# Moving a router's maximum and normalisation to later steps of a two-product expert kernel, with four banks for the second product in two steps

## The chip, the cores and the metric

The kernel runs on one core of one Trainium2 chip. The metric is the device time of one execution in microseconds (us); lower is better. TensorE is called PE below, VectorE DVE, ScalarE ACT, GpSimd POOL, and SyncE, which issues the DMAs, SP.

## What is computed

Attention feeds a layer with a cosine gate, and that feeds a mixture of eight experts whose router is normalised by rows and columns eight times. The change touches the last part:

```python
def _moe2_ref(x, w_gate, w1, w2):        # x 2304x512, w_gate 512x8, w1 8x512x1024, w2 8x1024x512
    logits = x @ w_gate
    logits = logits - logits.max()
    P = np.exp(logits)
    for _ in range(8):
        P /= P.sum(1, keepdims=True) + 1e-09
        P /= P.sum(0, keepdims=True) + 1e-09
        P *= N / E
    out = np.zeros((N, D))
    for e in range(E):
        h = np.maximum(x @ w1[e], 0.0)
        out += P[:, e:e + 1] * (h @ w2[e])
```

## The kernel before

**Steps.** The experts' part is a loop over 16 half-experts `u` (4 to 19) and three blocks of 768 tokens `j`. One pass is called a step here; step 0 is the first, so `s` is 12 plus the step, and there are 48. Three steps in a row, one for each `j`, make one half-expert; steps 0 to 5 are expert 0, steps 6 to 11 expert 1. A step has four groups `k` = 0 to 3 on PE. Each group starts with the first product of this step (x times w1; `g1_mult`, L763), in which seven multiplications stand for eight (Strassen's scheme): multiplications 0 and 6 in group 0, 1 and 5 in group 1, 4 and 3 in group 2, 2 in group 3. Then come the parts of the second product (h times w2; `g2_mult`, L837) of the step before. A multiplication is 12 matmuls of 384 columns, so a step has 7 x 12 of each product, 168 in all.

**PSUM banks.** The first product uses banks 0 to 3 in two pairs, X and Y (`two_banks(x)` and `two_banks(1 - x)`), which change roles with each step: what is Y in one step is X in the next, and the next step's first matmuls overwrite it. In group 3 only X is in use. The second product has two chains. With the table `WIDE` they use banks 4, 5 and 6, 7; with `NARROW` the second chain has bank 6 alone, so that bank 7 is free, and its parts 5, 3 and 2 are cut in halves of six matmuls. Between two halves bank 6 has to be read out (`g2_add`, L857 on DVE, or L859 on ACT where a block is written for the first time).

**Order.** Each engine works through its instructions in the order in which the code is written. Beside the two products the following ran in the first steps. `x_steps` (steps 0 to 2) makes the high and low halves of the seven combinations of x on ACT and DVE (`x_low` is L670, `x_sum` L652). `split_h` makes the halves of h (ACT L741, DVE L746), `first_sums`, `second_sum` and `third_sum` are L812, L817, L821. Group 3 adds a term to X (L805), then rectifies it on ACT.

**The router.** `logits` (matmuls L923, transposes L931, sums L911) and `sinkhorn` are generators. Each call of `step_side()` runs one of them to its next `yield`. Before the change there are four calls in every group: at its start, in the middle of its first product (`between`), and after its first and second part of the second product. `sinkhorn` takes the maximum `mx` (L939), transposes it on PE into bank 7 (L943), reduces it to `top` (L945), spreads it with a matmul (L949) and takes the exponentials (L952). One of the eight normalisations is: row sums `rs` and their reciprocals (DVE L956 to L958), their use and the column sums `cs` (L960, L964), a matmul with ones (L969) that adds them over the partitions, reciprocals `rc` (L971, L972) and their use (L974). At the end `by_e` (L979) is transposed on PE (L985) and stored to DRAM (`pd`).

**The use of the router.** `pb_load` (L886) reads 768 of these factors from `pd` into one of three tiles `pb`, spread over the partitions, on SP's queue. Expert 0 is multiplied with them after its second product (`scale_first`, L892, four DVE instructions per block, in steps 5 to 7); the experts after it at the rectification on DVE (`relu_scaled`, L775), from step 6 on.

**The end.** In the last step `out_tile` (L897 transposes into bank 7, L903 copies out) runs twice after all parts of groups 0, 1 and 2.

Of the kernel before, what the change touches and what calls it, by code (L numbers as in the profile page):

```python
# [18 lines left out]
P = 128  # L19
# [5 lines left out]
U1 = 2048 // 512  # L25
U2 = E * FE // 512
NU = U1 + U2
HC = 288

HT = 384  # L30
NJ = 3
# [73 lines left out]
def tile_kernel(ctx: ExitStack, tc: tile.TileContext, qT, kT, v, pT, w_in, w_out, w_gate, w1, w2, out):  # L105
    nc = tc.nc
# [718 lines left out]
    def split_h(s, m):  # L825
        h_high(s, m)
        h_low(s, m)
# [53 lines left out]
        for r, d in outs:  # L881
            g2_add(j, r, d, banks[chain], tiles)

    def pb_load(e, j):
        row = e * NT + 2 * HT * j
        nc.sync.dma_start(out=pb[j], in_=p_flat[row:row + 2 * HT].partition_broadcast(P))  # L886

    def scale_first(j, k):
        r, d = k // 2 + 1, k % 2 + 1
        scale = pb[j][:, HT * (2 - r):HT * (3 - r)].unsqueeze(1).to_broadcast([P, 2, HT])  # L890
        block = out_block(j, r, d)
        nc.vector.tensor_tensor(out=block, in0=block, in1=scale, op=ALU.mult)  # L892

# [12 lines left out]
    def out_tile(j, i, b):  # L906
        out_turn(j, i, b)
        out_store(j, i, b)
# [7 lines left out]
    def logits():  # L916
        copies = (l_sb, raws[4][:, 0:HT])
        for c in range(2 * NJ + 1):
            if c < 2 * NJ:
                ps = bank[:, 6 + c % 2, :]  # L920
                x = acc_cols(HT * c, HT)
                for k in range(KD):
                    nc.tensor.matmul(  # L923
                        ps[32 * k:32 * k + 32, 0:HT], lhsT=wgs[:, k, :], rhs=x[:, k, :],
                        start=True, stop=True,
                    )
                nc.scalar.copy(copies[c % 2], ps[:, 0:HT])
            if c > 0:
                ps, l = bank[:, 7 - c % 2, :], copies[1 - c % 2]
                for i in range(TQ):  # L930
                    nc.tensor.transpose(ps[:, P * i:P * i + P], l[:, P * i:P * i + P], ident)  # L931
                lg_sum(lg[:, TQ * c - TQ:TQ * c, :], ps, TQ)
            yield
            if c < 2 * NJ:
                yield

    def sinkhorn():
        mx = small.tile([P, 1], F32, tag="mx", name="mx")
        nc.vector.tensor_reduce(mx, lg, axis=AX.XY, op=ALU.max)  # L939
        yield  # L940
        yield
        t_ps = bank[:, 7, :]
        nc.tensor.transpose(t_ps[0:1, 0:P], mx, ident)  # L943
        top = small.tile([1, 1], F32, tag="top", name="top")
        nc.vector.tensor_reduce(top, t_ps[0:1, 0:P], axis=AX.X, op=ALU.max, negate=True)  # L945
        yield
        yield
        b_ps = bank[:, 7, :]
        nc.tensor.matmul(b_ps[:, 0:1], lhsT=ones[0:1, :], rhs=top, start=True, stop=True)  # L949
        nmx = small.tile([P, 1], F32, tag="nmx", name="nmx")  # L950
        nc.vector.tensor_copy(nmx, b_ps[:, 0:1])
# [2 lines left out]
        for k in range(8):  # L954
            rs = small.tile([P, NT // P], F32, tag="rs", name="rs")
            nc.vector.tensor_reduce(rs, prob, axis=AX.X, op=ALU.add)  # L956
            nc.vector.tensor_scalar(rs, rs, EPS, None, ALU.add)
            nc.vector.reciprocal(rs, rs)  # L958
            yield
            nc.vector.tensor_tensor(  # L960
                out=prob, in0=prob, in1=rs.unsqueeze(2).to_broadcast([P, NT // P, E]), op=ALU.mult
            )
            cs = small.tile([P, E], F32, tag="cs", name="cs")
            nc.vector.tensor_reduce(cs, prob.rearrange("p t e -> p e t"), axis=AX.X, op=ALU.add)  # L964
            yield
            yield
            yield
            c_ps = bank[:, 7, :]
            nc.tensor.matmul(c_ps[:, 0:E], lhsT=ones, rhs=cs, start=True, stop=True)  # L969
            rc = small.tile([P, E], F32, tag="rc", name="rc")  # L970
            nc.vector.tensor_scalar(rc, c_ps[:, 0:E], EPS, None, ALU.add)  # L971
            nc.vector.reciprocal(rc, rc)  # L972
            yield
            nc.vector.scalar_tensor_tensor(  # L974
                out=prob, in0=prob, scalar=float(NT) / E,
                in1=rc.unsqueeze(1).to_broadcast([P, NT // P, E]), op0=ALU.mult, op1=ALU.mult,
            )
# [19 lines left out]
    def step_side():  # L997
        while side:
            try:
                next(side[0])  # L1000
                return
            except StopIteration:
                side.pop(0)

    with tc.manual_schedule():
# [188 lines left out]
        for u in range(U1, NU):  # L1194
            for j in range(NJ):
                s = NJ * u + j
                first_unit = u == U1
                narrow = s <= NJ * U1 + 4 or s == NJ * NU - 1
                banks = ((4, 5), (6, 6)) if narrow else ((4, 5), (6, 7))
                if pair_no and not narrow:  # L1200
                    banks = banks[::-1]
                x = counts["chunk"] % 2
                counts["chunk"] += 1
                for k in range(4):
                    def between():
                        if prev is not None and k == 1:
                            h_low(s - 1, 3)
                        if NJ * (U1 + 1) + 2 <= s < NJ * (U1 + 2) + 2:
                            scale_first(s - NJ * (U1 + 1) - 2, k)
                        step_side()  # L1210

                    step_side()
                    if prev is not None:
                        if k == 0:
                            split_h(s - 1, 5)
# [7 lines left out]
                    if k == 2:  # L1223
                        first_sums(u, j, x)
                    parts = (NARROW if narrow else WIDE)[k] if prev is not None else ()
                    if prev is None and k < 3:
                        in_g2(n1 - 3 + k)
                        in_acc(n1 - 3 + k)
                        if k == 2:
                            split_h(s, 1)  # L1230
                    for n in range(max(2, len(parts))):
                        if n < len(parts):
                            g2_part(*prev, parts[n], banks)
                            if n == 0:
                                if k == 0:
                                    split_h(s - 1, 6)
                                elif k == 1:
                                    split_h(s - 1, 7)
                                    split_h(s - 1, 2)
                                elif k == 2:  # L1240
                                    split_h(s, 1)
                        if n < 2:
                            step_side()
                            if first_unit and 2 * k + n < 7 and 7 * j + 2 * k + n + 3 < 7 * NJ + 2:
                                x_steps(7 * j + 2 * k + n + 5, [halves(t) for t in pb])
                    if s == NJ * NU - 1 and k < 3:
                        out_tile(0, 2 * k, 7)
                        out_tile(0, 2 * k + 1, 7)

                    if first_unit and j == 0:  # L1250
                        for _ in range((2, 1, 0, 0)[k]):
                            next(preps[u], None)
# [2 lines left out]
                    if u + 1 < NU:  # L1255
# [7 lines left out]
                        if j == 2 and k == 3:  # L1263
                            makes[u + 1] = t_make(u + 1)
                            next(makes[u + 1])
                    if s == NJ * (U1 + 1) + 1 and k == 3:
                        for i in range(NJ):
                            pb_load(0, i)
                    if NJ * (U1 + 1) + 2 <= s < NJ * (U1 + 2) + 2:
                        if k == 3:  # L1270
                            pb_load(1, s - NJ * (U1 + 1) - 2)
                    if u >= U1 + 3 and k == 0:
                        if j > 0 and u % 2 == 1 and (u - U1) // 2 + 1 < E:
                            pb_load((u - U1) // 2 + 1, j - 1)
# [87 lines left out]
```

## Time and profile before

| | us |
|---|---|
| median of 3 runs | 1864.05 (1863.54 to 1865.42) |
| the profiled execution, its own time | 1863.85 |
| its span | 1861.8 |
| PE busy in the span | 1817.7 |
| DVE busy | 1482.7 |
| ACT busy | 829.5 |
| POOL busy | 834.3 |

The span runs from the first to the last instruction; 2.05 us of the execution's time lie outside it. A busy share is a mean over stages, and matmuls overlap, so what counts for PE is how long a step of 168 matmuls takes.

### The profile page before, as it was taken

How to read it: one execution, taken by the hardware profiler on the slowest of the kernel's cores; microseconds unless marked ns; L12 is line 12 of the kernel's file. 1: busy time of each engine (PE TensorE's matmuls, PEld its weight loads, DVE VectorE, ACT ScalarE, POOL GpSimd, SP SyncE). 2: the span in 40 equal slices, each digit the busy share in tenths (PEclk: the TensorE clock that was granted, in tenths of full speed). 3: DMA queues.
4: the chain of work that ended last, by engine and by line, in shares of the span. 5: the costliest groups of instructions: out<-in, count | busy, mean ns of one | idle time of the engine just before them, and what ended most of it. 6: DMA issues, size and time to landing. Idle time of an engine off the chain costs nothing.

```text
span 1861.8 us, 29725 instructions
## 1 busy us (share of the span) xinstructions
PE 1817.7 (98%) x11751; PEld 1775.0 (95%) x11751; DVE 1482.7 (80%) x1614; ACT 829.5 (45%) x1247; POOL 834.3 (45%) x542
## 2 busy tenths in 40 slices
PE   6999999997999999999999999999999999999998
PEld 4799999987899999999999999999999999999998
DVE  5867777558777988888888888888888888888876
ACT  5877777655544333333333333333333333333333
POOL 3544555543344454454545454444444544545420
PEclk9999999998999999999999999999999999999999
DMA  8511111035556766766766666666767666666652
GB/s 290 182 47 46 57 47 58 9 119 175 178 189 234 239 217 218 238 199 213 236 219 209 209 227 221 218 207 220 235 211 233 228 210 218 209 228 224 210 185 104
DMA packets 220839, 345.20 MB, mean 185 GB/s; under 512 B 13836, under 2 KB 190748, under 8 KB 220700
## 3 DMA queue, kind: packets, MB, share of 16 engines
q1 hardware_dynamic: 220700, 343.29, 55.4%
q8 instruction: 94, 1.54, 0.3%
q14 instruction: 45, 0.37, 0.1%
HBM read 321.93 MB, written 21.31 MB: 184 GB/s over the span
## 4 chain that ended last, share of the span: by engine, by line
PE 92%; DVE 4%; ACT 1%; issue 1%; DMA 1%; POOL 0%; ACTq 0%; SPq 0%; DVEq 0%; POOLq 0%
PE bank L837 37%; PE bank L763 36%; PE bank L606 11%; PE bank L547 2%; PE bank L548 2%; PE bank L549 2%; DMA k<-kT 1%; PE bank L483 1%; DVE hreg L746 1%; DVE xl L670 0%; PE bank L897 0%; DVE acc L857 0%; PE bank L308 0%; DVE pb L652 0%; ACT acc L859 0%
## 5 line engine op out<-in xcount | busy, mean ns | idle before, releaser
L837 PE MATMUL bank<-hreg,thi 128*128 128x384 f32 x2016 | 516.8, 337 | 6.7 <-DVE acc L857 5.0
L763 PE MATMUL bank<-xl,xh 128*128 128x384 f32 x1344 | 453.1, 337 | 3.8 <-DVE xl L670 3.8
L763 PE MATMUL bank<-xh 128*128 128x384 f32 x1344 | 454.7, 338 | 0.0
L763 PE MATMUL bank<-xh,xl 128*128 128x384 f32 x1344 | 452.7, 337 | 0.0
L857 DVE TENSOR_TENSOR acc<-bank,acc 128x768 f32<-128x768 f32 (+1 forms) x344 | 314.6, 916 | 116.6 <-PE bank L837 113.9
L837 PEld LDWEIGHTS bank<-hreg,thi 128*128 128x128 f32 x2016 | 366.6, 188 | 8.2 <-DVE acc L857 5.9
L746 DVE TENSOR_TENSOR hreg<-raw,hreg 128x768 fp32r<-128x768 f32 x252 | 337.4, 1346 | 23.6 <-ACT hreg L741 23.6
L837 PE MATMUL bank<-hreg,tlo 128*128 128x384 f32 x1008 | 340.0, 337 | 0.0
L741 ACT CAST hreg<-raw 128x768 fp32r<-128x768 f32 x252 | 207.3, 835 | 275.7 <-DVE raw L821 129.3
L243 POOL TENSOR_TENSOR tlo<-raw,thi 128x512 fp32r<-128x512 f32 x112 | 169.1, 1515 | 262.7 <-ACT thi L242 242.5
L813 POOL TENSOR_TENSOR raw<-raw,raw 128x768 f32<-128x768 f32 x48 | 88.8, 1851 | 399.4 <-DVE raw L812 399.4
L763 PEld LDWEIGHTS bank<-xl,xh 128*128 128x128 f32 x1344 | 253.8, 189 | 5.1 <-DVE xl L670 5.1
L763 PEld LDWEIGHTS bank<-xh 128*128 128x128 f32 x1344 | 253.3, 188 | 0.6 <-issue 0.6
L763 PEld LDWEIGHTS bank<-xh,xl 128*128 128x128 f32 x1344 | 253.5, 189 | 0.0
L711 POOL TENSOR_TENSOR xl<-wraw,xh 128x512 fp32r<-128x512 f32 x112 | 189.0, 1700 | 130.2 <-ACT xh L710 130.2
L837 PEld LDWEIGHTS bank<-hreg,tlo 128*128 128x128 f32 x1008 | 189.8, 188 | 0.0
L606 PE MATMUL bank<-hreg,whi 128*128 128x288 f32 x1024 | 187.9, 295 | 0.2 <-DVE rbuf L587 0.2
L775 DVE SCALAR_TENSOR_TENSOR raw<-bank,pb 128x768 f32<-128x768 f32 x168 | 160.0, 952 | 21.0 <-PE bank L763 16.5
L837 PE MATMUL bank<-slot,thi 128*128 128x384 f32 x672 | 172.6, 338 | 0.7 <-DVE acc L857 0.7
L606 PEld LDWEIGHTS bank<-hreg,whi 128*128 128x128 f32 x1024 | 153.1, 188 | 2.0 <-DVE rbuf L587 1.1
L242 ACT CAST thi<-raw 128x512 fp32r<-128x512 f32 x112 | 68.1, 619 | 156.6 <-POOL raw L246 155.2
L563 POOL TENSOR_TENSOR hreg<-rbuf,hreg 128x576 fp32r<-128x576 f32 x64 | 91.9, 1438 | 96.3 <-ACT hreg L557 86.7
(153 smaller groups left out, 2680.5 us busy)
## 6 DMA issues: line engine op xcount, KB each, us to landing
xh<-xd SPq DMA_DIRECT2D x315, 384.0 KB, 3.4
xl<-xd SPq DMA_DIRECT2D x315, 384.0 KB, 4.1
raw<-w SPq DMA_DIRECT2D x32, 512.0 KB, 6.3
wraw<-w SPq DMA_DIRECT2D x30, 512.0 KB, 6.2
pb<-pd SPq DMA_DIRECT2D x24, 384.0 KB, 5.6
raw<-w_in SPq DMA_DIRECT2D x16, 512.0 KB, 4.4
raw<-w_out SPq DMA_DIRECT2D x16, 512.0 KB, 3.7
xd<-xh SPq DMA_DIRECT2D x21, 384.0 KB, 3.1
```

Of the source, the lines that this page charges most:

```text
L242: nc.scalar.copy(hi, src)
L243: nc.gpsimd.tensor_tensor(out=lo, in0=src, in1=hi.bitcast(F32), op=ALU.subtract)
L563: nc.gpsimd.tensor_tensor(out=lo, in0=r, in1=hi.bitcast(F32), op=ALU.subtract)
L606: nc.tensor.matmul(ps[:, di, 0:HC], lhsT=lhsT, rhs=rhs, start=(n in (0, 6)), stop=(n in (17, 23)),)
L711: nc.gpsimd.tensor_tensor(out=lo, in0=src, in1=hi.bitcast(F32), op=ALU.subtract)
L741: nc.scalar.copy(hi, step_tiles(s)[H_SRC[m]])
L746: nc.vector.tensor_tensor(out=lo, in0=step_tiles(s)[H_SRC[m]], in1=hi.bitcast(F32), op=ALU.subtract)
L763: nc.tensor.matmul(dst, lhsT=w, rhs=t[:, k, :], start=start and k == 0 and w is a and t is th, stop=k == 1 and w is bq, skip_group_check=True,
L775: nc.vector.scalar_tensor_tensor(out=out, in0=src, scalar=0.0, in1=scale, op0=ALU.max, op1=ALU.mult)
L813: nc.gpsimd.tensor_tensor(out=r21, in0=r11, in1=r21, op=ALU.subtract)
L837: nc.tensor.matmul(dst, lhsT=w, rhs=t[:, p, :], start=start and p == 0 and w is a and t is hh, stop=p == 1 and w is bq, skip_group_check=True,
L857: nc.vector.tensor_tensor(out=dst, in0=src, in1=dst, op=ALU.add)
```

## The change

1. **Fewer calls.** `step_side()` runs four times per group only in step 0 and from step 3 on (`busy`); in steps 1 and 2 it runs once, in the middle of group 3. The number of yields is changed to match: the logits take all of step 0, `mx` is reduced in group 3 of step 0, its transpose and `top` stand in group 3 of step 1, the spreading and the exponentials in group 3 of step 2. The eight normalisations have four calls each instead of five, so that they fill steps 3 and 4, one per group; `by_e` is copied, transposed and stored in group 0 of step 5. The column sums now have two calls between them and their matmul, where they had three.
2. **Banks.** The transposed and the spread maximum go to the first bank of Y (`free["bank"]`), which group 3 does not use. `NARROW` now stands for steps 3, 4, 5 and the last instead of 1 to 4 and the last.
3. **Step 0.** The last three `in_g2` (the end of the layer before) move from ahead of both side calls of a group to between them.
4. **Factors.** The loads of `pb` and the scalings move to steps 5 to 8, with one load more (7 instead of 6), and group 2 has two scalings.
5. **The end.** The two `out_tile` of a group follow one part each.

```diff
-    def scale_first(j, k):
+    def scale_first(j, k, t):
...
-            yield
-            if c < 2 * NJ:
+            for _ in range((2, 2, 2, 2, 3, 1, 0)[c]):
                 yield
...
+    free = {}
...
-        yield
-        yield
-        t_ps = bank[:, 7, :]
+        for _ in range(4):
+            yield
+        t_ps = bank[:, free["bank"], :]
...
             cs = small.tile([P, E], F32, tag="cs", name="cs")
             nc.vector.tensor_reduce(cs, prob.rearrange("p t e -> p e t"), axis=AX.X, op=ALU.add)
-            yield
             yield
             yield
             c_ps = bank[:, 7, :]
...
-                narrow = s <= NJ * U1 + 4 or s == NJ * NU - 1
+                narrow = s in (NJ * U1 + 3, NJ * U1 + 4, NJ * U1 + 5, NJ * NU - 1)
...
+                    now = s - NJ * U1
+                    busy = now == 0 or now >= NJ
...
-                        if NJ * (U1 + 1) + 2 <= s < NJ * (U1 + 2) + 2:
-                            scale_first(s - NJ * (U1 + 1) - 2, k)
+                        if 2 * NJ <= now < 3 * NJ:
+                            for n in ((0,), (1,), (2, 3), ())[k]:
+                                scale_first(now - 2 * NJ, n, pb[(2, 2, 0)[now - 2 * NJ]])
+                        if busy or k == 3:
+                            free["bank"] = 2 * (1 - x)
+                            step_side()
+
+                    if busy:
                         step_side()
...
-                    if prev is None and k < 3:
-                        in_g2(n1 - 3 + k)
-                        in_acc(n1 - 3 + k)
-                        if k == 2:
-                            split_h(s, 1)
                     for n in range(max(2, len(parts))):
+                        if n == 1 and prev is None and k < 3:
+                            in_g2(n1 - 3 + k)
+                            in_acc(n1 - 3 + k)
+                            if k == 2:
+                                split_h(s, 1)
...
                         if n < 2:
-                            step_side()
+                            if s == NJ * NU - 1 and k < 3:
+                                out_tile(0, 2 * k + n, 7)
+                            if busy:
+                                step_side()
...
-                    if s == NJ * (U1 + 1) + 1 and k == 3:
-                        for i in range(NJ):
-                            pb_load(0, i)
-                    if NJ * (U1 + 1) + 2 <= s < NJ * (U1 + 2) + 2:
-                        if k == 3:
-                            pb_load(1, s - NJ * (U1 + 1) - 2)
+                    for when, group, e, i, t in (
+                        (5, 3, 1, 0, 0), (5, 3, 0, 0, 2), (5, 3, 1, 1, 1), (6, 2, 0, 1, 2),
+                        (7, 0, 0, 2, 0), (7, 2, 1, 2, 2), (8, 2, 1, 0, 0),
+                    ):
+                        if (now, k) == (when, group):
+                            pb_load(e, i, pb[t])
```

The lines below show what stands on an engine in the built program, first before and then after the change; line numbers are those of each kernel. On DVE, at the end of step 1, from the readout of part 2 on (`acc` L857; `xl` and `pb` are the splitting of x, `rs`, `rc`, `prob`, `cs` the router's), before:

```order
L971 TENSOR_SCALAR rc<-bank 128x8
L972 RECIPROCAL rc<-rc 128x8
L670 TENSOR_TENSOR xl<-pb_3999,xh 128x2x384
L652 TENSOR_TENSOR pb_3998<-acc_1628,pb_3997 128x768
L857 TENSOR_TENSOR acc_101<-bank,acc_101 128x384
L974 SCALAR_TENSOR_TENSOR prob<-prob,rc 128x144
L956 TENSOR_REDUCE rs<-prob 128x18
L957 TENSOR_SCALAR rs<-rs 128x18
L958 RECIPROCAL rs<-rs 128x18
L805 TENSOR_TENSOR bank<-bank,base 128x2x384
L960 TENSOR_TENSOR prob<-prob,rs 128x144
L964 TENSOR_REDUCE cs<-prob 128x8
```

And after, at the same place, up to the first two instructions of step 2:

```order
L857 TENSOR_TENSOR acc_101<-bank,acc_101 128x2x384
L670 TENSOR_TENSOR xl<-pb_3999,xh 128x2x384
L652 TENSOR_TENSOR pb_3998<-acc_1628,pb_3997 128x768
L805 TENSOR_TENSOR bank<-bank,base 128x2x384
L948 TENSOR_REDUCE top<-bank 1x1
L670 TENSOR_TENSOR xl<-acc_1628,xh 128x2x384
L746 TENSOR_TENSOR slot<-raw_4411,slot 128x768
L817 TENSOR_TENSOR raw_4411<-raw_4411,raw_4408 128x768
```

The normalisation's instructions are gone from there, and the reduction to `top`, which reads the first bank of Y, stands behind L805. On SP's queue, at the end of step 5 (`xh`, `xl` are loads of x, `raw32` loads of w2, `pb` the factors), before:

```order
L682 DMA xh_73<-xd_94 128x2x384
L682 DMA xl_74<-xd_94 128x2x384
L218 DMA raw32_6026<-w2 128x2x512
L218 DMA raw32_6028<-w2 128x2x512
L886 DMA pb0_3997<-pd_4416 128x768
```

And after:

```order
L682 DMA xh_73<-xd_94 128x2x384
L682 DMA xl_74<-xd_94 128x2x384
L218 DMA raw32_6014<-w2 128x2x512
L218 DMA raw32_6016<-w2 128x2x512
L886 DMA pb0_3997<-pd_4416 128x768
L886 DMA pb2_3999<-pd_4416 128x768
L886 DMA pb1_3998<-pd_4416 128x768
```

Three loads of factors stand there instead of one. The second of them, `pb2`, is read by the first scaling of step 6, which stands on DVE after the change as follows (its line is now L894):

```order
L746 TENSOR_TENSOR slot_4407<-raw5_4411,slot_4407 128x768
L817 TENSOR_TENSOR raw5_4411<-raw5_4411,raw2_4408 128x768
L894 TENSOR_TENSOR acc0_101<-acc0_101,pb2_3999 128x2x384
L791 TENSOR_TENSOR bank_81<-bank_81,raw0_4000 128x2x384
L857 TENSOR_TENSOR acc1_1628<-bank_81,acc1_1628 128x2x384
L746 TENSOR_TENSOR hreg_83<-raw5_4411,hreg_83 128x768
```

Before, a scaling stood at this place too (L892), with `pb1`, which was loaded in step 4.

## Rows read from the trace of the kernel before

**Rows 1.** The page: the chain of work that ended last, by engine.

```profile
PE 92%; DVE 4%; ACT 1%; issue 1%; DMA 1%; POOL 0%; ACTq 0%; SPq 0%; DVEq 0%; POOLq 0%
```

**Rows 2.** Steps 0-4, 7, 8: length; PE, PEld, DVE, ACT, POOL busy; PEclk; DMA.

```profile
386.92:424.93 38.01, 32.31 (x220) 26.98 (x216) 20.23 (x27) 16.92 (x28) 18.38 (x12) 0.99 0.32 114
424.93:469.49 44.56, 37.68 (x178) 35.63 (x178) 34.70 (x53) 23.68 (x34) 14.05 (x8) 0.86 0.45 157
469.49:506.72 37.23, 32.85 (x178) 31.32 (x176) 29.14 (x47) 19.34 (x29) 14.32 (x9) 0.95 0.56 184
506.72:540.52 33.80, 30.54 (x177) 29.90 (x176) 25.22 (x38) 17.07 (x26) 14.44 (x9) 1.00 0.57 186
540.52:569.85 29.33, 29.33 (x169) 29.33 (x169) 21.37 (x23) 14.49 (x20) 11.37 (x8) 1.00 0.66 224
...
628.54:657.87 29.33, 29.33 (x170) 29.33 (x170) 28.36 (x30) 11.41 (x16) 13.16 (x9) 1.00 0.73 240
657.87:687.18 29.31, 29.31 (x169) 29.31 (x169) 27.41 (x25) 10.57 (x15) 17.17 (x10) 1.00 0.62 203
```

**Rows 3.** PE's waits in steps 0 to 3: total us, times, longest us.

```profile
PE bank L837 <- DVE acc L857: 5.6, 3, 2.8
PE bank L763 <- DVE xl L670: 3.8, 4, 2.6
PE bank L985 <- DVE by_e L979: 3.2, 1, 3.2
PE bank L943 <- DVE mx L939: 3.1, 1, 3.1
PE bank L923 <- DVE acc L617: 1.8, 1, 1.8
...
PE bank L923 <- DVE lg L911: 0.8, 2, 0.4
```

**Rows 4.** Busy time by stretch, behind three of PE's waits; PEclk is the granted clock.

```profile
424.90:431.00 6.10, 6.10 (x20) 5.65 (x21) 3.87 (x4) 5.00 (x7) 4.55 (x3) 0.51 0.55 198
...
492.40:496.00 3.60, 3.60 (x12) 3.60 (x13) 3.57 (x6) 0.00 (x0) 0.00 (x0) 0.54 0.71 254
...
535.20:540.50 5.30, 5.30 (x32) 5.30 (x31) 2.61 (x4) 1.44 (x3) 1.30 (x1) 1.00 0.40 119
```

**Rows 5.** DVE in step 1, instructions that touch rs, rc or cs (busy, count).

```profile
424.93:469.49 44.56, 3.13 (x12) 0.86 0.45 157
...
424.93:469.49 44.56, 1.92 (x6) 0.86 0.45 157
...
424.93:469.49 44.56, 0.71 (x6) 1.04 (x6) 1.29 (x3) 0.86 0.45 157
```

**Rows 6.** Timeline, step 1: last matmul of multiplication 2, and DVE's L805.

```profile
462.10 0.34 PE L763 MATMUL bank<-xh,xl 128*128 128x384 f32 x1
...
466.07 0.94 DVE L805 TENSOR_TENSOR bank<-bank,base 128x768 f32<-128x768 f32 x1
```

**Rows 7.** Timeline, step 4, DVE: the third sum, and the low half of h3.

```profile
550.61 0.94 DVE L821 TENSOR_TENSOR raw<-raw,raw 128x768 f32<-128x768 f32 x1
552.46 0.96 DVE L746 TENSOR_TENSOR slot<-raw,slot 128x768 fp32r<-128x768 f32 x1 [0.90 <-ACT slot L741]
```

**Rows 8.** Loads of pb issued at 599.3 (one), 567.8-568.8 (three); DVE's scaling, step 6.

```profile
DMA to landing us min/median/max: 7.7/7.7/7.7
...
DMA to landing us min/median/max: 6.1/6.6/7.1
...
602.13 0.95 DVE L892 TENSOR_TENSOR acc<-acc,pb 128x768 f32<-128x768 f32 x1
```

**Rows 9.** Timeline: POOL and DVE side by side in step 2.

```profile
498.00 1.85 POOL L813 TENSOR_TENSOR raw<-raw,raw 128x768 f32<-128x768 f32 x1 [6.48 <-DVE raw L812]
...
498.31 2.35 DVE L746 TENSOR_TENSOR hreg<-raw,hreg 128x768 fp32r<-128x768 f32 x1
```

**Rows 10.** Timeline of PE in the last step: the second of two output tiles.

```profile
1810.30 0.33 PE L897 MATMUL bank<-ident,acc 128*128 128x128 f32 x1 [0.68 <-ACT rows L903]
```

More of the change, by code (lines that the diff above doesn't have):

```diff
@@ L882, in g2_part, with pb_load @@
             g2_add(j, r, d, banks[chain], tiles)
-    def pb_load(e, j):
+    def pb_load(e, j, t=None):
         row = e * NT + 2 * HT * j
-        nc.sync.dma_start(out=pb[j], in_=p_flat[row:row + 2 * HT].partition_broadcast(P))
-    def scale_first(j, k):
+        nc.sync.dma_start(
+            out=pb[j] if t is None else t, in_=p_flat[row:row + 2 * HT].partition_broadcast(P)
+        )
+    def scale_first(j, k, t):
         r, d = k // 2 + 1, k % 2 + 1
-        scale = pb[j][:, HT * (2 - r):HT * (3 - r)].unsqueeze(1).to_broadcast([P, 2, HT])
+        scale = t[:, HT * (2 - r):HT * (3 - r)].unsqueeze(1).to_broadcast([P, 2, HT])
         block = out_block(j, r, d)
@@ L946, in sinkhorn @@
         yield
-        yield
-        b_ps = bank[:, 7, :]
+        b_ps = bank[:, free["bank"], :]
         nc.tensor.matmul(b_ps[:, 0:1], lhsT=ones[0:1, :], rhs=top, start=True, stop=True)
@@ L964, in sinkhorn @@
             nc.vector.tensor_reduce(cs, prob.rearrange("p t e -> p e t"), axis=AX.X, op=ALU.add)
-            yield
             yield
@@ L1242, in tile_kernel @@
                         if n < 2:
-                            step_side()
+                            if s == NJ * NU - 1 and k < 3:
+                                out_tile(0, 2 * k + n, 7)
+                            if busy:
+                                step_side()
                             if first_unit and 2 * k + n < 7 and 7 * j + 2 * k + n + 3 < 7 * NJ + 2:
                                 x_steps(7 * j + 2 * k + n + 5, [halves(t) for t in pb])
-                    if s == NJ * NU - 1 and k < 3:
-                        out_tile(0, 2 * k, 7)
-                        out_tile(0, 2 * k + 1, 7)
                     if first_unit and j == 0:
```

## The prediction

> **What bounds the kernel now.** I read the chain of work first: 92% of what ended last is PE [rows 1], so a change counts by what it does to PE's time. Then I cut the experts' part into steps. From step 4 on a step takes 29.33 us with PE busy throughout, 0.1746 us for each of its 168 matmuls, while DVE is busy for 21 to 28 us of it [rows 2]. The first steps take longer: step 0 38.01, step 1 44.56, step 2 37.23, step 3 33.80 us. Steps 1 to 3 alone are 27.6 us above three times 29.33. That is what can be had, and the view of PE's waits says where it goes: 5.6 us for readouts of the second product's banks by DVE, 3.8 for low halves of x, 3.1 for the maximum, 3.2 for `by_e`, 1.8 and 0.8 in the logits [rows 3]. Nearly all end at DVE, which is busy for 34.70 us in step 1 and 29.14 in step 2 [rows 2].
>
> A wait can cost twice. After the 3.1 us for `mx`, PE ran 6.1 us at a granted clock of 0.51, which is nearly all at 1.2 of 2.4 GHz; after the longest wait for x (2.6 us) 3.6 us at 0.54. After `by_e` (3.2 us) the clock stayed at 1.00 [rows 4]. So a wait of two or three us sometimes, not always, costs half of the next 3.6 to 6 us more: 3.6 x 0.46 = 1.7, or 6.1 x 0.49 = 3.0.
>
> **The change, part by part.**
>
> *Step 0.* The wait for `mx` (3.1) goes: between its reduction and its transpose lies a step. The two waits for a sum of logits (0.8 together) go too, since an `in_g2` now lies between one sum and the matmul that overwrites its bank. The 1.8 for `acc` stays in kind: the last logits still stand right behind the last `in_g2`. But ACT and POOL get the work of group 1 earlier, so that DVE should be free when `in_g2` ends; I take 0.7 of it (between 0 and all 1.8, or 0.9 worse, if the `x_low` that now stands ahead is in the way). Sum: 3.1 + 0.8 + 1.1 = **-5.0**.
>
> *Step 1.* It loses the half-rate start (3.0), DVE's normalisation instructions and the halves of parts 5, 3 and 2. The normalisation is 3.13 + 1.92 + 1.29 = 6.34 us of DVE in this step [rows 5], or about 2.4 for one round of eight. DVE keeps 34.70 - 6.34 = 28.4 us of work. Two bounds: PE's own 29.3, and DVE's work with all its idle time of before (44.56 - 34.70 = 9.9), 38.3. The end of the step decides where between. Before, L805 began at 466.07, 3.6 us after multiplication 2 had ended (462.10 + 0.34) [rows 6]: DVE was that late. Behind L805 now stands `top`, which reads the first bank of Y, and the next step's first matmul overwrites just this bank. What covers it is part 4, 12 matmuls or 2.1 us; L805 and a short reduction take 1.3, so DVE may be 0.8 us late for nothing, and each us beyond that stops PE. DVE still has the seven splittings of x in this step. I take 34.0, a wait of some 3 us for `top` and 1 to 2 us of waits for low halves: **-10.6** (from -6.3 to -15.2).
>
> *Step 2.* DVE's 29.14 lose three rounds (7.3), and only four of seven splittings of x are left: 21.9 of work, with all the idle time of before (8.1) 30.0. The spread maximum has the same place as `top`, with DVE no longer late. PE's 29.3, about 0.2 for a low half and one fall of the clock after the wait for `top` (1.7) make 31.2: **-6.0** (-4.5 to -7.9).
>
> *Step 3.* `by_e` (3.2) goes; the rounds it has anyway rise from two to four. 29.3, four column-sum matmuls of about 0.14, and 1.1 for waits: 31.0, **-2.8** (0 to -3.9).
>
> *Step 4* is new ground: 21.37 us of DVE work [rows 2] plus four rounds, 9.7, is 31.1, over the 29.33 of PE. Where it bites is read from group 1. The third sum began at 550.61 and the low half of h3 at 552.46 [rows 7]. Now `cs`, `rc`, and the next `rs` stand ahead of the third sum, 2.1 us at best, so the low half comes near 554.8 to 555.7, and the next `cs` behind it ends near 556.4. Its matmul stands behind 84 others, at 540.52 + 84 x 0.1746 = 555.2: a wait of 1.3. Group 3 comes out alike. With the four matmuls: **+3.1** (0.6 to 8).
>
> *Step 5.* Two transposes, and `by_e` is ready 6 us earlier than its turn: **+0.3**.
>
> *Step 6.* At the end of step 5 the queue holds two loads of w2 and now three of factors. The one at this place took 7.7 us to land, and three in a row landed 1.0 us apart (567.8 + 6.1, then 568.8 + 7.1) [rows 8]. So `pb0` lands at 607.0 of the old clock, and `pb2`, the second, at 608.0. The scaling that reads `pb2` ran at 602.13 [rows 8]: DVE will stand still for 5.9 us, with the add into Y and the readout of part 1 behind it. Multiplication 5 needs that add at 599.20 + 60 x 0.1746 = 609.7; it comes at 608.0 + 2 x 0.95 = 609.9. Then come a readout, the low half of h6, a readout and the third sum, some 4 us, so that this sum is there at 614.0, while part 3, due at 599.20 + 84 x 0.1746 = 613.9, needs two halves made of it, 1.8 more. 0.2 + 1.9 and a little for what is late behind them: **+2.5** (0, if the load lands 4 us sooner, to 5.9).
>
> *Steps 7 and 8.* DVE had 28.36 and 27.41 us of work; step 7 keeps its four scalings, step 8 gets four (3.8) and has 31.2, over PE's 29.3. What step 6 leaves behind can't be made up. **+1.3** (0 to 4).
>
> Here the Trainium skill speaks against the change. The row first: L746 usually takes 0.95 us, but 2.35 when POOL's L813 had begun 0.31 us earlier [rows 9]; it ended 0.81 us after POOL did. The page "SBUF — State Buffer", section "SBUF: two separate sides", says that DVE instructions with two SBUF inputs and POOL share one port pair under an exclusive lock, and that the loser blocks for the whole instruction; the trace agrees. By it alone each of the twelve scalings could take 1.85 us longer, 22 us of DVE in steps 6 to 8 and about the whole gain.
>
> *The end.* The second of two output tiles waited 0.68 us for the copy of the first [rows 10], three times; a part of the second product now lies between: **-2.0**.
>
> The sum: -5.0 - 10.6 - 6.0 - 2.8 + 3.1 + 0.3 + 2.5 + 1.3 - 2.0 = -19.2. The profiled execution took 1863.85 (span 1861.8 and 2.05 around it), 0.2 below the median, 1864.05. That gives **1844.7**.
>
> **Rivals.**
>
> *All is hidden.* Step 1 goes to 30.0 and step 2 to 29.6, step 3 to 30.3, and steps 4 to 8 cost nothing: -5.0 - 14.6 - 7.6 - 3.5 - 2.0 = -32.7, **1831**. For it: DVE's mean over steps 0 to 8 is some 26 us per step. Against it: L805's lateness and the load of `pb2`.
>
> *DVE bounds steps 4 to 8.* If DVE cannot give up the 2 to 3 us of waits that it has in a full step, step 4 costs 4.7, step 6 5.9, steps 7 and 8 4.5 together; with +0.3 that is 15.4 in place of 7.2: **1853**. For it: the waits of DVE for ACT's high halves are in its path [rows 7]. Against it: step 7 ran with 28.36 us of DVE and no wait of PE. The rule of the page "SBUF — State Buffer" in the Trainium skill leads to this case, and at its worst, with each scaling held, to 1844.7 + 22 = 1867; [rows 9] show such a hold, but not that every instruction meets one.
>
> *Slower: the column sums.* Each of the eight matmuls with ones stops PE until DVE has done `cs`, and now has one call less of distance. Should each cost what `by_e` cost, 3.2, and a fall of the clock, 1.7, eight are 39 in place of my 2.6: **1881**. The point from which it decides is 2.8 us for each (19.2 + 2.6 over 8). Against it: the eight of before waited hardly at all, in a DVE as full as that of step 3 will be.
>
> *No change.* The first steps are set by the chain from ACT to DVE to PE for the splitting of x, not by the normalisation: step 1 stays at 40, step 2 at 35, and the third case holds too: 1844.7 + 6.0 + 3.8 + 8.2 = **1863**.
>
> **How the numbers follow.** The forecast has 0.62, all hidden 0.12, DVE's bound 0.20, no change 0.03, slower 0.03. The range of 8 in 10 reaches into the second and third case: 1836 to 1854. A measurement of this kernel tells about 0.2% (3.7 us) from no change; all of the first three cases are faster by more. Faster 0.94, same 0.03, slower 0.03.
>
> **What would show it.** Step 0 near 33 us with no wait for `mx`; step 1 near 34, its longest wait at the first matmul of step 2, ended by the reduction to `top`; no waits for second-product banks in steps 1 and 2; short waits for `cs` in step 4; DVE idle for about 6 us in front of the first scaling of step 6, ended by a DMA; 29.3 us from step 9 on. I am wrong if step 1 stays above 38, if step 4 or 6 takes over 36, or if a matmul for a column sum waits more than 3 us.

## The result and the profile after

The changed kernel took 1848.28 us (median of 4 runs, 1845.22 to 1849.0) against 1864.74 for the kernel before (4 runs): a ratio of 0.9907, 95% interval 0.9889 to 0.9924. It is faster by about 0.9%; forecast were 1844.7 us, 19.2 us less than the profiled execution of before. The profiled execution after took 1848.91 us, its span is 1846.6: 14.9 us less in time, 15.2 in the span.

The view of busy time by stretch, one row per step (start:end, length, then PE, PEld, DVE, ACT and POOL busy with counts, granted clock, DMA share and GB/s), steps 0 to 4 and 6 to 8 of the changed kernel, answers to [rows 2]:

```profile
386.97:419.15 32.18, 32.00 (x218) 26.95 (x215) 18.58 (x25) 17.02 (x27) 16.59 (x11) 1.00 0.36 129
419.15:454.05 34.90, 30.26 (x171) 29.08 (x170) 29.18 (x29) 20.49 (x29) 14.65 (x10) 0.98 0.60 205
454.05:488.34 34.29, 32.71 (x170) 32.13 (x171) 22.85 (x22) 20.90 (x30) 14.97 (x10) 0.92 0.56 182
488.34:522.09 33.75, 31.23 (x177) 30.12 (x177) 27.08 (x47) 17.65 (x28) 13.29 (x9) 1.00 0.64 210
522.09:554.10 32.01, 30.75 (x178) 30.12 (x178) 29.93 (x56) 13.20 (x19) 10.21 (x7) 1.00 0.62 206
...
583.77:614.99 31.22, 30.24 (x170) 29.20 (x169) 25.64 (x25) 9.09 (x13) 11.23 (x7) 1.00 0.78 255
614.99:644.68 29.69, 29.60 (x169) 29.27 (x169) 28.69 (x30) 11.39 (x16) 13.24 (x9) 1.00 0.73 244
644.68:674.00 29.32, 29.32 (x169) 29.32 (x169) 28.95 (x26) 10.46 (x15) 16.62 (x11) 1.00 0.62 200
```

Steps 0 and 1 gave 5.8 and 9.7 us, step 2 gave 2.9, step 3 nothing (0.05); steps 4 and 6 took back 2.7 and 1.9. The stretch from the start of the last step to the end went from 60.1 (1801.69 to 1861.8) to 57.8 us. PE's waits from step 0 to step 9 (total us, times, longest us) answer to [rows 3]:

```profile
PE bank L763 <- DVE top L948: 3.4, 1, 3.4
PE bank L837 <- DVE acc L857: 2.4, 4, 1.3
PE bank L763 <- DVE xl L670: 1.8, 2, 1.6
PE bank L970 <- DVE cs L966: 1.2, 2, 0.6
PE bank L763 <- ACT raw L772: 1.0, 1, 1.0
PE bank L837 <- DVE hreg L746: 0.6, 1, 0.6
PE bank L763 <- DVE bank L791: 0.3, 1, 0.3
PE bank L837 <- ACT acc L859: 0.3, 1, 0.3
```

The waits for `mx`, `by_e`, the logits and `acc` L617 are gone. A wait for `top` is new and now the longest. The timeline shows it, PE and DVE at the end of step 1:

```profile
454.05 0.69 PE L763 MATMUL bank<-xh 128*128 128x384 f32 x1 [3.44 <-DVE top L948]
...
450.92 2.01 DVE L652 TENSOR_TENSOR pb<-acc,pb 128x768 f32<-128x768 f32 x1
452.86 0.95 DVE L805 TENSOR_TENSOR bank<-bank,base 128x768 f32<-128x768 f32 x1
453.72 0.27 DVE L948 TENSOR_REDUCE top<-bank 1x1 f32<-1x128 f32 x1
```

DVE came to L805 and to `top` only after the last splitting of x, and the first matmul of step 2 started 0.06 us after `top` ended. In step 6, DVE's timeline reads:

```profile
585.83 0.96 DVE L817 TENSOR_TENSOR raw<-raw,raw 128x768 f32<-128x768 f32 x1
592.06 1.69 DVE L894 TENSOR_TENSOR acc<-acc,pb 128x768 f32<-128x768 f32 x1 [5.28 <-DMA pb<-pd]
593.67 0.95 DVE L791 TENSOR_TENSOR bank<-bank,raw 128x768 f32<-128x768 f32 x1
```

and the view of `pb`'s three loads, issued at 583.4 to 584.4, gives their times from issue to landing:

```profile
DMA to landing us min/median/max: 6.8/8.1/8.7
```

DVE stood still for 5.28 us in front of the first scaling; 5.9 were forecast.

### The profile page after: what moved, and what is told of

It is laid out like the page before. It is cut to its first block, busy times and chain, and to the rows that moved or that the text cites. A ratio compares the mean times of both kernels' runs of the same rounds, so it can differ in the third digit from the quotient of the medians.

```text
span 1846.6 us, 29714 instructions
## 1 busy us (share of the span) xinstructions
PE 1814.5 (98%) x11751; PEld 1770.5 (96%) x11751; DVE 1479.4 (80%) x1613; ACT 828.2 (45%) x1243; POOL 831.4 (45%) x542
## 4 chain that ended last, share of the span: by engine, by line
PE 89%; DVE 6%; ACT 2%; issue 1%; DMA 1%; POOL 1%; SPq 0%; ACTq 0%; DVEq 0%; POOLq 0%
PE bank L763 35%; PE bank L837 35%; PE bank L606 11%; PE bank L547 2%; PE bank L549 2%; PE bank L548 2%; DVE hreg L746 1%; DVE acc L857 1%; DMA k<-kT 1%; PE bank L483 1%; DMA pb<-pd 0%; DVE slot L746 0%; DVE xl L670 0%; PE bank L899 0%; ACT raw L772 0%
## 5 line engine op out<-in xcount | busy, mean ns | idle before, releaser
L857 DVE TENSOR_TENSOR acc<-bank,acc 128x768 f32<-128x768 f32 (+1 forms) x343 | 313.4, 916 | 113.1 <-PE bank L837 110.7
L746 DVE TENSOR_TENSOR hreg<-raw,hreg 128x768 fp32r<-128x768 f32 x252 | 332.2, 1326 | 22.6 <-ACT hreg L741 22.5
```

The lines of the kernel that those rows point to most:

```text
L746: nc.vector.tensor_tensor(out=lo, in0=step_tiles(s)[H_SRC[m]], in1=hi.bitcast(F32), op=ALU.subtract)
L857: nc.vector.tensor_tensor(out=dst, in0=src, in1=dst, op=ALU.add)
```

## Experiments

My theory after the result: the gain is the sum of named waits, and what is left of it in steps 1 to 6 is DVE coming late to an instruction that PE needs, for three reasons: the splittings of x ahead of L805 and `top` (step 1), the rounds of the normalisation (steps 3 and 4), and a load (step 6). The rival throughout: DVE is simply too full, so that time taken away at one place comes back at the next. Nine kernels change one thing each of the changed kernel; two runs follow them. Single runs are compared by the lengths of their steps, since most steps that an edit does not touch agree within 0.1 us. Step 2 does not: with the same instructions in it, it took 30.6 to 34.3 us, and a large part of that is the granted clock (run 11). Half rate below means its lower level, 1.2 of 2.4 GHz; the clock of each row has to be read beside its length. Step 6 took 31.2 to 31.5 us in most runs, but 31.9 in run 7, whose edit does not touch it.

**1. The maximum in group 2.**

```diff
-                        if busy or k == 3:
-                            free["bank"] = 2 * (1 - x)
+                        if busy:
                             step_side()
...
-                            if busy:
+                            if busy or (n == 1 and k == 2):
+                                free["bank"] = 2 * (1 - x)
                                 step_side()
```

> The transpose and the spreading of the maximum move from group 3 to the end of group 2 in steps 1 and 2, so that the reduction to top stands ahead of the last four or five DVE instructions of the step. Theory (the wait at the first matmul of step 2 is only the place of top in DVE's order): the wait of 3.4 us and the 17 matmuls at half rate behind it (2.6 us) go, step 2 falls from 34.3 to 28.5 to 30 us, step 1 stays near 34.9, the whole by 4.5 to 6 us. Rival (DVE with its splitting of x is late whatever stands there): the time comes back as waits for low halves of x or for banks in step 2, which stays above 32.5; the whole falls by less than 2 us.

1845.97 us. The wait for `top` went, but steps 1 and 2 together fell only from 69.2 to 66.8 us (31.27, and 35.56 at a granted clock of 0.95), and another wait took its place. The timeline of this kernel, PE, ACT and DVE at the start of step 2:

```profile
454.51 0.45 PE L763 MATMUL bank<-xh 128*128 128x384 f32 x1 [2.02 <-ACT raw L772]
...
453.65 0.81 ACT L772 ACTIVATE raw<-bank 128x768 f32<-128x768 f32 x1 [5.07 <-DVE bank L805]
...
452.66 0.95 DVE L805 TENSOR_TENSOR bank<-bank,base 128x768 f32<-128x768 f32 x1
```

Multiplication 6 overwrites the old X, which L772 rectifies after L805 has added to it. L805 came as late as before (452.66, then 452.86), so the theory's narrow form, that only the place of `top` matters, is wrong; what is late is L805, and the wait for `top` hid it.

**2. One bank for the second chain in steps 1 and 2 again.**

```diff
-                narrow = s in (NJ * U1 + 3, NJ * U1 + 4, NJ * U1 + 5, NJ * NU - 1)
+                narrow = NJ * U1 < s <= NJ * U1 + 5 or s == NJ * NU - 1
```

> The changed kernel with one bank for the second chain in steps 1 and 2 again. Theory (banks and normalisation each give a part): the waits for the readout of bank 6 come back, 3 to 6 us in steps 1 and 2 together, since DVE is 3 to 4 us late at the end of step 1. Rival (with the normalisation away the readouts are in time): steps 1 and 2 stay within 0.7 us of 34.9 and 34.3.

1852.38 us; steps 1 and 2:

```profile
419.18:459.57 40.39, 33.66 (x170) 31.79 (x170) 30.97 (x32) 22.05 (x32) 14.77 (x10) 0.92 0.55 189
459.57:491.69 32.12, 31.01 (x172) 29.47 (x172) 23.07 (x24) 20.96 (x31) 15.70 (x9) 1.00 0.58 192
```

72.5 against 69.2 us for both. The waits for readouts of the second product came back with 6.3 us, a little more than the 3 to 6 of the theory; the two steps grew by 3.3 us only, since the wait for `top` went. Step 1 alone is 5.5 longer and step 2 2.2 shorter; this is in part a shift of the half rate, which here lies in step 1 (0.92) and in the changed kernel's first profile in step 2 (0.92).

**3. The factors earlier.**

```diff
+                    if (now, k) == (5, 2):
+                        for e, i, t in ((0, 0, 2), (1, 0, 0), (1, 1, 1)):
+                            pb_load(e, i, pb[t])
...
-                        (5, 3, 1, 0, 0), (5, 3, 0, 0, 2), (5, 3, 1, 1, 1), (6, 2, 0, 1, 2),
+                        (6, 2, 0, 1, 2),
```

> The three loads of factors are issued in group 2 of step 5, ahead of the two loads of w2, with the one that step 6 needs first in front. Theory (step 6 is long because DVE stands still for a load): DVE's idle time before the first scaling goes, step 6 falls from 31.2 to 29.4 to 29.7 us and step 7 to 29.3; the whole falls by 1.9 to 2.4. Rival (DVE is too full in steps 6 to 8): step 6 stays above 30.7.

1842.83 us. Steps 6 and 7, by stretch, and then DVE's first scaling in the timeline:

```profile
580.10:609.45 29.35, 29.35 (x170) 29.35 (x169) 25.85 (x25) 9.20 (x13) 11.03 (x7) 1.00 0.69 227
609.45:638.87 29.42, 29.42 (x169) 29.30 (x169) 28.40 (x30) 11.41 (x16) 12.94 (x9) 1.00 0.75 250
```

```profile
583.04 0.95 DVE L894 TENSOR_TENSOR acc<-acc,pb 128x768 f32<-128x768 f32 x1
```

Step 6 is 1.9 shorter and step 7 0.3: the load was the cause. The scaling runs 2.9 us into the step without a wait, as it did before the change. Another 3.7 us of this run's gain lie in step 2, which the edit does not touch; run 11 deals with that.

**4. No rounds.** The eight normalisations are left out, so that the factors are the plain exponentials.

```diff
-        for k in range(8):
+        for k in range(0):
             rs = small.tile([P, NT // P], F32, tag="rs", name="rs")
```

> The eight normalisations are left out (the factors are the plain exponentials), all else stays. Theory (step 3 and 4 are long because of the rounds on DVE): step 3 falls from 33.7 to 29.7 to 30.7, step 4 from 32.0 to 29.3 to 29.7. Rival (the halves of parts 5, 3 and 2 in one bank and the first writes by ACT make step 3 long): step 3 stays above 32, step 4 falls to 29.4.

1837.29 us; steps 3 and 4:

```profile
488.34:518.59 30.25, 30.03 (x171) 29.36 (x171) 16.81 (x19) 17.67 (x28) 14.03 (x9) 1.00 0.71 234
518.59:547.82 29.23, 29.23 (x169) 29.21 (x169) 21.38 (x23) 14.48 (x20) 11.36 (x8) 1.00 0.66 218
```

6.3 us less in both, and PE has no wait in them that the view of waits lists. The rounds cost that; the single bank without them can cost 0.9 us in step 3 (30.25 against 29.33) and nothing in step 4. The whole fell by more than that, since step 2 took 33.0 us here and most steps behind step 5 29.2 instead of 29.32; why they did is not shown.

**5. The second bank of Y.**

```diff
-                            free["bank"] = 2 * (1 - x)
+                            free["bank"] = 2 * (1 - x) + 1
```

> The maximum is transposed and spread in the second bank of Y instead of the first. The next step's multiplication 0 writes the first bank with its first six matmuls and the second with its last six. Theory (the wait for top is the overwriting of its bank): the wait moves to the seventh matmul of step 2 and falls from 3.4 to 2.4 us. Rival (DVE's lateness stops the step in another place as well): the wait at the first matmul stays at 3 us or more, with another instruction of DVE or ACT as its releaser. The half rate behind the wait may come or not; it is told apart from the wait.

1846.13 us. PE's timeline, step 2:

```profile
454.37 0.44 PE L763 MATMUL bank<-xh 128*128 128x384 f32 x1 [2.29 <-DVE top L948]
```

The step began at 450.86, so the wait is now 1.2 us into it, at its seventh matmul, and 1.15 us shorter. The wait is the overwriting of that bank.

**6. The output tiles together.** `out_tile` stands twice behind the parts of a group again.

```diff
-                            if s == NJ * NU - 1 and k < 3:
-                                out_tile(0, 2 * k + n, 7)
...
+                    if s == NJ * NU - 1 and k < 3:
+                        out_tile(0, 2 * k, 7)
+                        out_tile(0, 2 * k + 1, 7)
```

> Only the output tiles of the last step go back to the end of each group. Theory: three waits of 0.68 us come back, the stretch from the start of the last step to the end grows from 57.8 to 59.9 us, all steps before it stay. Rival (the time before came from elsewhere in the tail): under 0.5 us of difference.

1848.40 us; the stretch from the start of the last step to the end took 60.5 instead of 57.8. (The whole shows nothing of it, since step 2 took 31.8 us at a clock of 1.00 here.) PE's waits in its first groups came back:

```profile
PE bank L899 <- ACT rows L905: 2.0, 3, 0.7
```

The order of the tiles is worth 2.6 us (57.83 and 60.47 unrounded), not 2.0: more than the waits alone.

**7. `in_g2` ahead of the calls.**

```diff
-                        if n == 1 and prev is None and k < 3:
+                        if n == 0 and prev is None and k < 3:
```

> In step 0 the last three in_g2 stand ahead of both side calls again; the rest as changed. Theory (my term for step 0: 3.1 for the maximum, the rest, 2.7 us of it, for this order): step 0 grows from 32.2 to between 33.5 and 34.9 us, with waits for sums of logits of 0.4 us each and one for acc. Rival (all of step 0 came from the maximum and the spread calls): step 0 stays within 0.4 us of 32.2.

1855.34 us; steps 0 and 1:

```profile
387.99:422.77 34.78, 32.11 (x218) 27.09 (x215) 16.98 (x22) 16.74 (x27) 16.06 (x11) 1.00 0.26 93
422.77:460.97 38.20, 31.69 (x171) 30.64 (x170) 31.77 (x33) 20.58 (x29) 14.81 (x10) 0.94 0.61 212
```

Step 0 is 2.6 longer, as expected, and step 1 is 3.3 longer, which I had not expected: the wait for L772 at its start is 3.0 instead of 1.0 us, and in the 6 us behind it the granted clock was 0.72, which is 1.7 us more. So this small change of order is worth some 6 us between these two profiles, more than any of its own waits; 1.7 of them are the clock, which differs from run to run.

**8. The last splitting of group 2 behind L805 and `top`, in steps 0 and 1.**

```diff
-                            if first_unit and 2 * k + n < 7 and 7 * j + 2 * k + n + 3 < 7 * NJ + 2:
-                                x_steps(7 * j + 2 * k + n + 5, [halves(t) for t in pb])
+                            q = 2 * k + n - (j < 2 and k == 3)
+                            if first_unit and q < 7 and 7 * j + q + 3 < 7 * NJ + 2:
+                                if not (j < 2 and k == 2 and n == 1):
+                                    x_steps(7 * j + q + 5, [halves(t) for t in pb])
```

> In steps 0 and 1 the splitting of x that stands last in group 2 (one low half and one difference on DVE, 1.6 + 2.0 us in step 1) moves behind L805 and top into group 3. Theory (what stops step 2 is how late DVE comes to L805, top and the rectification behind it, and the splittings ahead make it late): DVE comes to L805 some 3 us sooner, the wait for top falls from 3.4 to under 0.7 and nothing takes its place, steps 1 and 2 together fall from 69.2 to between 62 and 65.5 us, and the 1.0 us at the start of step 1 goes too. Rival (the work only changes places): a wait for a low half of x or for h5 of 2 us or more takes its place in step 2, steps 1 and 2 stay above 67.

1845.76 us; steps 1 and 2 by stretch, and then DVE's timeline at the end of step 1:

```profile
420.48:452.88 32.40, 30.90 (x170) 29.00 (x169) 27.95 (x29) 20.57 (x29) 10.67 (x8) 1.00 0.57 189
452.88:485.39 32.51, 31.05 (x170) 29.51 (x171) 26.58 (x24) 21.54 (x31) 18.51 (x11) 1.00 0.70 230
```

```profile
451.69 0.95 DVE L805 TENSOR_TENSOR bank<-bank,base 128x768 f32<-128x768 f32 x1
452.56 0.27 DVE L948 TENSOR_REDUCE top<-bank 1x1 f32<-1x128 f32 x1
```

64.9 us for both instead of 69.2. There is no wait for `top` or L772 any more, and none of over 0.9 us in these steps; so what made those waits is DVE's lateness behind the splittings, as the theory's second form has it. What that is worth is another matter. The 69.2 us hold the half rate behind `top`; in runs 3 and 6, where the wait for `top` was 3.4 us too but the clock stayed at 1.00, the same two steps took 65.5 and 66.6 us. Against these the edit gives 0.6 to 1.7 us, and the rival's mark of 67 us can't tell the theories apart. Against run 3, waits of PE in these steps fell from 5.0 to 2.9 us (what is left are eight small ones, for low halves of h and x), while PE was busy for 1.5 us longer (61.95 against 60.43) with as many matmuls, which no run explains. So most of the time did come back, as the rival says, in small pieces.

**9. The third call of a round again.**

```diff
             nc.vector.tensor_reduce(cs, prob.rearrange("p t e -> p e t"), axis=AX.X, op=ALU.add)
             yield
             yield
+            yield
             c_ps = bank[:, 7, :]
```

> The changed kernel with the third call between the column sums and their matmul again, so that a normalisation has five calls and the eight end in group 2 of step 5. Theory (steps 3 and 4 are long because DVE has four rounds in each, and the waits for cs are only where this shows): step 3 and 4 fall from 65.8 to between 63 and 64.5 us together, as a fifth of the rounds leaves them, step 5 grows from 29.7 to 30 to 31, and waits for a bank of the second product stay. Rival (the one call less of distance is what costs): the waits for cs (1.2 us) go and steps 3 to 5 together fall by 1.2 us or more with the other waits as they were.

1852.23 us. Both theories fail: the waits for `cs` went, but steps 3 and 4 grew from 65.8 to 69.0 us, step 5 from 29.7 to 31.2. Of the 3.2 us in steps 3 and 4, 1.7 are a stretch at half rate behind the longest wait (granted clock 0.95 in step 3). The timeline, PE and then DVE in step 3:

```profile
518.13 0.65 PE L837 MATMUL bank<-hreg,thi 128*128 128x384 f32 x1 [4.00 <-DVE acc L857]
...
512.51 1.39 DVE L976 SCALAR_TENSOR_TENSOR prob<-prob,rc 128x144 f32<-128x144 f32 x1
513.93 0.30 DVE L958 TENSOR_REDUCE rs<-prob 128x18 f32<-128x144 f32 x1
514.27 0.78 DVE L959 TENSOR_SCALAR rs<-rs 128x18 f32<-128x18 f32 x1
515.08 0.27 DVE L960 RECIPROCAL rs<-rs 128x18 f32<-128x18 f32 x1
515.27 0.89 DVE L857 TENSOR_TENSOR acc<-bank,acc 128x768 f32<-128x768 f32 x1
516.08 1.09 DVE L962 TENSOR_TENSOR prob<-prob,rs 128x144 f32<-128x144 f32 x1
517.21 0.41 DVE L966 TENSOR_REDUCE cs<-prob 128x8 f32<-128x144 f32 x1
517.53 0.55 DVE L857 TENSOR_TENSOR acc<-bank,acc 128x384 f32<-128x384 f32 x1
```

With five calls a round no longer stands at the same place in every group, and here six of its instructions (4.2 us) came to stand ahead of the readout of half of part 2, for which the other half waits. So in steps 3 and 4 it is not the number of rounds alone that counts, but what of a round stands ahead of a half's readout.

**10. Runs 3 and 8 together**, timed.

> The splitting behind top (steps 0 and 1) and the earlier loads of factors together. Theory (the two costs are of different steps and add): steps 1 and 2 together 65, steps 6 and 7 together 58.8 us; against the changed kernel -4.3 (or -1.8 in executions whose clock did not fall behind the wait for top) and -2.1, so 1841 to 1844 us. Rival (what is taken away in step 6 or 2 comes back in a neighbour): over 1846.

1843.41 us (median of 4, 1841.94 to 1844.09), ratio 0.9883, 0.9869 to 0.9898. Steps 1 and 2 took 65.0, 6 and 7 58.8 us, each pair what it took with its own edit alone. The changed kernel, timed beside it (run 11), took 1846.71, so the combination is 3.3 us faster than it. Run 3 showed 2.1 us of this in steps 6 and 7; some 1.2 are left for the edit of run 8. The single time of run 3, 1842.83, lies inside the combination's range, so the times alone do not show that the second edit adds to the first.

**11. The changed kernel once more**, timed.

> The changed kernel itself, for a second profile and times beside those of the combination. Theory (the clock behind the wait for top falls in some executions only): times between 1845 and 1849 us in two groups some 2.5 us apart; the profile shows a wait of 3.4 us in front of step 2 with step 2 either near 34 or near 31.8 us long. Rival (the half rate belongs to the wait): step 2 again 34.3 us.

1846.71 us (median of 4, 1845.77 to 1850.28), ratio 0.9907, 0.9891 to 0.9924. Step 2 took 32.25 us, neither of the two values expected. Three stretches of 6 us behind the wait for `top` (3.4, 3.7 and 3.4 us long), from the first profile of the changed kernel, this second one, and run 3, show why. Each stands in a fence of its own, the last one with the row of run 3's whole step 2:

```profile
454.05:460.00 5.95, 5.95 (x20) 5.95 (x21) 3.43 (x3) 4.08 (x6) 3.26 (x3) 0.54 0.38 137
```

```profile
453.85:459.85 6.00, 6.00 (x25) 6.00 (x26) 3.48 (x3) 4.07 (x6) 3.26 (x3) 0.72 0.37 132
```

```profile
453.94:459.90 5.96, 5.96 (x34) 5.96 (x35) 3.44 (x3) 4.80 (x7) 3.28 (x3) 1.00 0.38 137
453.94:484.58 30.64, 30.19 (x170) 29.61 (x171) 22.99 (x22) 20.81 (x30) 15.84 (x10) 1.00 0.63 204
```

The same wait was followed by 20, 25 or 34 matmuls in 6 us, at a mean granted clock of 0.54, 0.72 or 1.00, that is by a long, a short or no stretch at 1.2 GHz. Runs 4, 6, 7 and 9 have this wait too (3.4 to 3.7 us): behind it the clock was 0.55 in runs 4 and 7, and 1.00 in runs 6 and 9. The half rate does not belong to the wait; up to some 2.7 us of a run of this kernel are decided by it (0.46 of 5.95 us).

## Why the prediction was right

The mechanism was right at most places, though not in step 3, and the time lies within the range. That the sum came within 3.8 us is in part luck: steps 1 to 3 missed by 6.8 us in one direction, and the other terms by 3.0 in the other. By its own terms:

| term | forecast | measured |
|---|---|---|
| step 0 | -5.0 | -5.8 |
| step 1 | -10.6 | -9.7 |
| step 2 | -6.0 | -2.9 |
| step 3 | -2.8 | -0.05 |
| step 4 | +3.1 | +2.7 |
| step 5 | +0.3 | +0.3 |
| step 6 | +2.5 | +1.9 |
| steps 7, 8 | +1.3 | +0.4 |
| the end | -2.0 | -2.3 |
| sum | -19.2 | -15.4 |

(Step 9 adds 0.2 to the measured sum, which gives the 15.2 us of the span.)

*Step 0* gained what was named, and 0.8 more: the wait for `acc`, of which 0.7 was to stay, went whole. Run 7 shows the share of the order: 2.6 us here. That it also relieves step 1, by 3.3 us in that run, was in no term. *Step 1* came out 0.9 us short. The wait for `top` was forecast at some 3 us and was 3.44; its price is shown by run 5 as that of a bank, and run 8 shows that DVE's lateness behind the splittings makes it. In place of 1 to 2 us of waits for low halves there was one of 0.2, and a wait of 1.0 for L772, which was in no term: these two nearly cancel. Nor did the forecast have that L772 of the next step is held up by the same lateness as `top` (run 1).

The clock had a larger part in the gain than the forecast gave it. It took 3.0 us of half rate out of step 1 and put 1.7 into step 2. By the granted clock of [rows 2], 0.86 over 44.56 us and 0.95 over 37.23, half rate cost the kernel before some 6.2 and 1.9 us in steps 1 and 2; in the changed kernel's first profile it was 2.7 us, in step 2. So some 5 of the 12.6 us that the two steps gave are the clock, an estimate from these rows. All eight timed executions of the changed kernel have a mean granted clock of 0.995 to 0.998, seven of the kernel before, timed beside run 11, one of 0.991 to 0.995.

*Step 2* is the term that was mis-sized most, by 3.1 us. The half rate behind `top` cost some 2.7 instead of 1.7, and one low half of x cost 1.58 instead of 0.2:

```profile
477.42 0.44 PE L763 MATMUL bank<-xl,xh 128*128 128x384 f32 x1 [1.58 <-DVE xl L670]
...
475.29 2.07 DVE L670 TENSOR_TENSOR xl<-pb,xh 128x768 fp32r<-128x768 f32 x1
...
475.26 3.26 POOL L711 TENSOR_TENSOR xl<-wraw,xh 128x512 fp32r<-128x512 f32 x2 [1.58 <-ACT xh L710]
```

That splitting took 2.07 instead of 0.95 us, and POOL had begun 0.03 us before it, much as in [rows 9]. The page "SBUF — State Buffer" of the Trainium skill, section "SBUF: two separate sides", says that whichever of the two starts first holds the shared ports until it ends and the other waits; the trace agrees here, 2.07 against 0.95; in run 3 POOL began first too, by 0.02 us, and DVE took 0.95 (last section). In runs 3 and 11 these waits for low halves were 0.6 us in all. Both parts of the error vary from run to run: step 2 took 30.64 us in run 3, 32.25 in run 11, 34.29 in the first profile, with the same instructions in it. The remaining 0.7 us of the error have no cause shown; run 3, with neither part, still took some 0.9 us more than PE's 29.3 and its wait of 0.45.

*Step 3* is the other, by 2.8 us. Four rounds were priced at 1.1 us of waits and 0.6 of matmuls; run 4 shows that the rounds make 3.5 of the step's 33.75, and that without them the step takes 30.25, not the 29.3 that the sum began with. With the rounds 1.9 of the step's 2.5 us of waits are waits for the single bank, without them there are none, and run 9 shows that a round makes them by standing ahead of a readout. I had looked for the cost only at `cs`. *Step 4* was priced by DVE's work over PE's, and the size held (2.7, forecast 3.1); the path did not. In place of two waits of 1.3 us for `cs` there was one of 0.62, and one of 0.63 for a readout; the rest is PE's own busy time, 30.75 us with the rounds and 29.23 without (run 4).

*Step 6* was right in its cause (run 3) and nearly in its size, though its second wait, for a half of h, was 0.55 us where 1.9 were forecast. *Steps 7 and 8* cost less: DVE was busy for 28.95 us in step 8, not 31.2, and PE waited for nothing. The rival that DVE bounds steps 4 to 8 is refuted for 6 to 8 by run 3, where they take 29.4 us each with all twelve scalings. Nor was each scaling held: in the changed kernel's first profile eight of the twelve took 0.95 us, one 1.69 and three 2.05, some 4 us more in all, not 22. For step 4 it is open: DVE was busy for 29.93 of 32.01 us, over PE's 29.33, but the step cost 2.7, not 4.7. The rival of the column sums is out: two waits, 1.2 us. That all is hidden would have needed what run 8 does, and more.

## What to carry over

A scratch result in a bank that is idle now still has a deadline: the next writer of that bank; look at what the reading engine has ahead of the reader, not at how short it is. When a wait ends at a late engine, moving the one instruction that PE waits for only shows the next one behind it (run 1); moving the bulk of work in front of them takes the waits away (run 8). But on an engine with little to spare most of the time comes back elsewhere: 4.4 us of waits went there, and 0.6 to 1.7 us were gained where the clock was the same. Read the granted clock of both profiles before you price a wait by the length of a step: here a stretch at half rate, which comes behind the same wait in some runs only, was worth up to 2.7 us behind a wait of 3.4. Side work in an in-order engine should not stand ahead of a readout that frees a single buffer; how many calls it is cut into decides where it comes to stand, and one call more cost 4.7 us in steps 3 to 5, 1.7 of them half rate (run 9).

## What the runs showed of the hardware that was not expected

After equal waits of 3.4 to 3.7 us at the same place in the same program, PE's granted clock over the next 6 us was 0.54, 0.72 or 1.00. Two more profiles gave 0.55, two more 1.00.

And when DVE and POOL began within 0.04 us of each other on SBUF operands, it was not always the same one that was held: in the first profile of the changed kernel DVE's L670 took 2.07 us and POOL's two instructions 3.26 together; in run 3 DVE's took 0.95 and POOL's two 4.11, though POOL had again begun first, by 0.02 us. The trace's start times, in nanoseconds, sort all twelve profiles of the changed kernel and its variants: in the four in which DVE was held (the first, runs 1, 6 and 9), POOL had begun 27 to 32 ns earlier; in the other eight it had begun 23 ns earlier at most, or later, and DVE took 0.95 us. So the order of the two starts went with who was held, with the border near 25 ns rather than at 0; whether the records of the two engines are shifted against each other by that much, no run here shows.
